# Twelve tile transposes go from TensorE to transfers on SyncE's queue, and one small product moves down the program order

## The chip, the cores and the metric

The kernel runs on one core of a Trainium2 chip. A core has five engines with instruction queues of their own: TensorE (PE in the profile, its weight loads PEld), VectorE (DVE), ScalarE (ACT), GpSimd (POOL) and SyncE (SP). Each queue is worked off in order; engines wait for one another through semaphores. Sixteen DMA engines move data between the large memory and the on-chip memory, or within the latter; SP, ACT and POOL only issue such transfers. TensorE writes to a small memory of eight banks (PSUM), from which VectorE or ScalarE copy. The metric is the device time of one execution in microseconds (us), less is better. Three executions before the change took 158.83, 157.96 and 158.57 us, with a median of 158.57.

## The reference

Two layers in a row, for 4 batches of 768 tokens, 8 heads of 64 and a model width of 512. The first is a recurrent attention with a decay per head:

```python
gamma = 1.0 - 2.0 ** (-5.0 - np.arange(H))
for t in range(S):
    state = gamma[None, :, None, None] * state + np.einsum('bhd,bhe->bhde', k[:, :, t], v[:, :, t])
    y[:, :, t] = scale * np.einsum('bhd,bhde->bhe', q[:, :, t], state)
```

Its output, with the heads side by side, is x of the second, a channel mix with a hidden width of 1024:

```python
xk = mu_k * x + (1.0 - mu_k) * x_prev      # x_prev: the token before
xr = mu_r * x + (1.0 - mu_r) * x_prev
k = np.maximum(xk @ w_k, 0.0)
v = k * k @ w_v
r = 1.0 / (1.0 + np.exp(-(xr @ w_r)))
return r * v
```

## The kernel before

The tokens are cut into 12 blocks of 256, three per batch: blocks 0 to 2 are batch 0, 6 to 8 batch 2, 9 to 11 batch 3. A block's attention is computed in chunks rather than token by token: masked scores of q and k inside a chunk, and products of q with the state carried from the chunks before. Blocks 0 to 5 use two chunks of 128 tokens, blocks 6 to 11 (`HALF`) four of 64.

The order of all work is written out by hand in `ORDER`. Each word is one step, `code.block.part`, with `~` the engine (v, a, p, s) and `@` the PSUM banks. The program emits the words from left to right, so each engine gets its instructions in that order. The words that matter here:

- `lq`, `lk`, `lv` load q, k, v of a block (`load`, lines 222 to 237, on POOL, which also casts q and k to 16 bits). They land in rings of four buffers, `Q16`, `K16`, `V32`, so a load waits until the block four places earlier has been read.
- `Tq`, `Tk` (`trans`, lines 264 to 283) transpose q and k on TensorE, so that the head's 64 features lie on the partitions. In blocks 6 to 11 that is 32 small products of 64x64 for each word (line 278). `Eq`, `Ek` (`turned_q`, `turned_k`, through `copy`, line 241) copy the outcome from PSUM to `QT`, `KT`, rings of three, on ScalarE.
- `S` scores (lines 310 to 343), `M` mask on VectorE (345 to 355), `C` the block's own states (357 to 399), `U` their sums with the carried state (`summed`, 419), `G` the decay (`decayed`, 421).
- `I`, `Y`, `J` the output products: `inter` (431 to 446, products at 441) with the carried state, called once for each half of the pairings, and `intra` with the masked scores (462, 478, 489). `HEADS` gives the pairs of heads that share the 128 partitions of `QT` and `KT`; the pairs (3, 2) and (7, 6) stand in turned order.
- `D` scales y into `xT` (507, 514), `dx` forms the differences of neighbouring tokens (529), `X` mixes them with the mu rows (538).
- `K` with `Qa`, `Qb`: the hidden layer on TensorE (552, 562) and its square on ScalarE (571, 579, 583). `V`: product with `w_v` (604). `R`, `s`: gate (592, 598). `O`: the result on VectorE into a ring of four `OS` buffers (610), `st`: its store on SP (617). An `O` therefore waits until the store of four half blocks earlier is done.
- `mu`, `mt`, `me`: the two mu vectors are loaded on ACT's queue (654), turned by one product on TensorE (`trans_mu`, 659), copied to `mu` on ScalarE (662).
- `z.n`: products of zeros (667, 674) that compute nothing.

Before the change SP's queue holds two early loads of block 0 and then only the 24 stores. The order around the start on TensorE is: the transposes of block 0, `mt`, two zero products, the first scores, the remaining k transposes, `C.0`, more scores, `Y.0`.

Of the kernel before, what the change touches and what calls it, by code (L numbers as in the profile page):

```python
# [33 lines left out]
X.1.1.3 X.1.1.2 Qb.1.0 Tq.3@1 Eq.3~a J.2 X.1.1.0 X.1.1.1 R.1.0@6 s.0.0 lk.3~p Tk.3@1 vs.3~v D.2~v
dx.2~v X.2.0.2 X.2.0.0 C.3@23 X.2.0.3 Ek.3~a s.1.0 X.2.0.1 lk.4~p U.3.0~a R.1.1@0 lq.4~p s.1.1
Tk.4@1 S.3.1@45 S.3.0@67 Qb.1.1 Qb.1.3 U.3.1 lv.4~p Tq.4@0 Ek.4~a Eq.4~a wv.0~p K.2.2@2 Qa.2.2
M.3.1~v K.2.0@3 Qa.2.0 G.3~a M.3.0~v K.2.3@1 vs.4~v Qb.0.3 S.4.1@45 S.4.0@67 M.4.0~v I.3@23
M.4.1~v Qa.2.3 lq.6~p lq.7~p K.2.1@0 Qb.2.0 Y.3 C.4@67 V.1.0.0@1 U.4.0 U.4.1 G.4~a I.4@45 J.3
Qa.2.1 D.3~v dx.3~v Y.4 V.1.1.0@6 Tq.7@23 J.4 D.4~v wv.1~p Qb.2.1 V.0.1.0@0 lk.6~p V.0.0.0@7
X.2.1.2 dx.4~v X.3.0.1 X.3.0.2 X.3.0.3 Eq.7~a V.1.1.1 X.3.0.0 V.0.0.1 O.0.0 Tk.6@45 Ek.6~a lq.5~p  # L40
Tq.6@23 lv.5~p Qb.2.2 V.0.1.1 Eq.6~a V.1.0.1 O.1.0 K.3.6@4 K.3.1@5 Qb.2.3 lk.5~p K.3.0@7 Qa.3.6
Tq.5@4 Qa.3.1 Qa.3.0 vs.5~v C.5@5 X.2.1.1 Eq.5~a Tk.5@1 Ek.5~a S.6@23 O.0.1 O.1.1 lk.7~p U.5.0
Tk.7@67 Ek.7~a X.2.1.0 I.5@45 M.6~v X.3.1.3 K.3.2@0 K.3.3@1 Qa.3.2 Qb.3.1 lv.6~p S.5.0@23 Qa.3.3
Qb.3.0 X.3.1.1 S.5.1@67 Qb.3.3 X.2.1.3 Qb.3.2 K.3.4@0 st.0.0 Qa.3.4 M.5.1~v lk.8~p K.3.5@1 Qa.3.5
R.2.1@6 lv.8~p lk.9~p s.2.1 M.5.0~v Y.5 S.7@23 Tk.8@01 Ek.8~a J.5 X.3.1.0 X.3.1.2 R.3.1@7 s.3.1
V.2.0.0@6 K.3.7@0 lv.7~p vs.6~v R.2.0@7 V.2.0.1 D.5~v M.7~v s.2.0 dx.5~v X.5.1.1 O.2.0 Qa.3.7
Qb.3.6 V.2.1.0@1 Tk.9@23 C.6@45 U.6.0~a Ek.9~a lq.8~p Tq.8@67 Qb.3.7 X.5.0.3 V.2.1.1 vs.7~v
R.4.0@0 Eq.8~a U.6.1 U.6.2 X.5.0.0 U.6.3 st.0.1 R.3.0@2 C.7@45 X.5.0.1 s.4.0 I.6@67 s.3.0 st.1.1
X.5.0.2 K.5.3@3 Qa.5.3 O.2.1 lq.10~p K.5.1@0 Qa.5.1 G.6~v X.5.1.3 V.3.0.0@1 U.7.0 U.7.1 U.7.2
st.2.1 I.7@23 Y.6 vs.8~v U.7.3 G.7~a lq.11~p R.4.1@0 D.6~v V.4.1.0@4 lv.11~p C.8@67 Y.7 V.3.1.0@5  # L50
Qb.5.1 Qb.3.4 Qb.3.5 V.3.0.1 dx.6~v s.4.1 U.8.0 U.8.1 V.3.1.1 Qb.5.3 D.7~v U.8.2 V.4.1.1 dx.7~v
X.6.0.1 X.6.0.3 V.4.0.0@7 K.5.0@6 X.5.1.2 X.6.0.2 Qa.5.0 V.4.0.1 Qb.5.0 K.5.2@0 X.6.0.0 Qa.5.2
Qb.5.2 X.6.1.2 lv.9~p K.6.7@6 Qa.6.7 st.2.0 st.1.0 O.4.1 O.3.0 K.6.0@2 Qa.6.0 lk.10~p O.4.0 O.3.1
st.3.1 K.6.4@0 S.8@67 I.8@23 Tk.10@45 Qa.6.4 K.6.1@1 Ek.10~a X.6.1.1 X.5.1.0 Qa.6.1 Qb.6.1 K.6.6@0
Qb.6.0 Qa.6.6 vs.9~v K.6.5@4 Qa.6.5 M.8~v R.5.1@1 Qb.6.6 Tq.10@67 Eq.10~a s.5.1 Y.8 Tq.11@45
Qb.6.7 lv.10~p vs.10~v X.6.1.3 Eq.11~a D.8~v dx.8~v lq.9~p X.8.0.2 X.8.0.1 lk.11~p R.5.0@0 s.5.0
K.6.3@6 Qa.6.3 V.5.1.0@7 Tq.9@23 X.6.1.0 Eq.9~a S.10@45 M.10~v Qb.6.3 C.9@01 U.9.0~v st.3.0 U.9.1
V.5.1.1 K.6.2@6 Qa.6.2 R.6.1@2 s.6.1 U.9.2 R.6.0@3 s.6.0 I.9@45 U.9.3 O.5.1 X.8.0.3 S.9@01 M.9~v
X.8.0.0 G.9~a C.10@67 U.10.0 U.10.1 Qb.6.2 vs.11~v R.7.1@2 s.7.1 V.5.0.0@3 Qb.6.5 st.4.1 Tk.11@01
Ek.11~a U.10.2 U.10.3 V.5.0.1 Qb.6.4 K.8.0@2 Qa.8.0 G.10~v I.10@01 Y.9 C.11@67 st.4.0 R.7.0@2  # L60
O.5.0 V.6.1.0@3 D.9~v U.11.0 U.11.1 s.7.0 K.8.3@4 Qa.8.3 V.6.1.1 U.11.2 I.11@67 st.5.0 dx.9~v
O.6.1 S.11@45 X.8.1.2 Y.10 V.7.1.0@2 M.11~v D.10~v dx.10~v X.9.0.3 X.9.0.2 X.9.0.1 V.7.0.0@3 Y.11
X.9.0.0 Qb.8.0 K.8.2@4 Qa.8.2 X.8.1.0 X.9.1.1 K.8.1@5 Qa.8.1 D.11~v V.6.0.0@0 V.7.0.1 V.6.0.1
K.9.3@1 K.9.7@5 Qa.9.7 X.8.1.1 V.7.1.1 X.8.1.3 dx.11~v K.9.2@4 O.7.0 Qb.8.1 Qb.9.7 O.6.0 Qa.9.3
st.5.1 Qa.9.2 X.11.1.0 Qb.8.3 X.11.0.3 K.9.1@5 K.9.4@6 st.7.0 Qa.9.1 Qb.9.1 R.8.0@1 s.8.0
V.8.1.0@3 Qb.9.2 X.9.1.0 K.9.0@0 Qa.9.0 Qb.8.2 X.9.1.2 Qb.9.3 K.9.6@1 Qa.9.6 Qb.9.6 O.7.1 st.7.1
K.9.5@7 Qa.9.5 V.8.0.0@0 X.11.0.2 X.11.0.1 Qb.9.0 X.11.0.0 K.11.3@2 K.11.0@1 Qa.11.3 st.6.1
R.8.1@5 V.8.1.1 X.11.1.2 Qa.9.4 st.6.0 X.9.1.3 R.9.1@2 R.10.1@4 R.10.0@6 V.8.0.1 O.8.0 s.8.1
K.11.1@5 Qb.9.4 s.10.0 V.9.0.0@7 V.9.1.0@0 Qa.11.1 Qb.11.1 O.8.1 Qb.9.5 Qb.11.3 Qa.11.0 st.8.1
K.11.2@6 Qa.11.2 V.10.1.0@5 Qb.11.2 Qb.11.0 V.9.1.1 R.9.0@1 X.11.1.3 s.9.0 X.11.1.1 V.9.0.1 O.9.0  # L70
st.9.0 V.11.0.0@6 s.10.1 s.9.1 O.9.1 st.9.1 V.10.0.0@1 V.10.1.1 O.10.1 st.8.0 st.10.1 V.11.0.1
R.11.0@0 s.11.0 O.11.0 V.10.0.1 R.11.1@7 s.11.1 O.10.0 st.10.0 Vc.11.1.1@0 Oc.11.1.1 Vc.11.1.0@6
st.11.0 sc.11.1.1~a Oc.11.1.0 sc.11.1.0~s
# [4 lines left out]
def kernel(  # L78
# [16 lines left out]
    P = 128  # L95
# [28 lines left out]
    gd_np = gam[np.array(HEADS).T[par // D]] ** TM  # L124
# [16 lines left out]
    Q16 = ring("q16_", 4, [H, 2 * D], F16)  # L141
    K16 = ring("k16_", 4, [H, 2 * D], F16)
# [16 lines left out]
    csm = const.tile([P, 4 * H + (2 + LOG) * NJ + 2 * NCO], F32, name="csm_sb")  # L159
# [14 lines left out]
    gd = csm[:, o : o + NJ]  # L174
# [22 lines left out]
    def heads(j):  # L197
        return [(a, h, h // 2, h % 2) for a, h in enumerate(HEADS[j])]

# [15 lines left out]
    def more(n):  # L215
        return n % NB < NB - 1

    def staged(a):
        f = K2(1 + a).rearrange("p f t -> p (f t)").bitcast(F32)
        return f[:, 0 : H * 2 * D].rearrange("p (h d) -> p h d", h=H)  # L220

    def load(x, d, split, a=None):
        def go(e, n, j0=0, j1=NJ):
            b, t0 = n // NB, n % NB * TM
            hs = slice(2 * j0, 2 * j1)
            src = x[b, hs, t0 : t0 + TM, :]
            dst = staged(a)[:, hs] if (a, n, j0) in EARLY else d(n)[:, hs]
# [536 lines left out]
```

## Time and profile before

| | |
|---|---|
| median of three executions | 158.57 us (157.96 to 158.83) |
| the profiled execution | 158.7 us from first to last instruction, its span |
| TensorE busy | 149.7 us, 94% |
| VectorE busy | 128.0 us, 81% |
| ScalarE busy | 98.9 us, 62% |
| GpSimd busy | 55.1 us, 35% (it issues the loads) |
| bytes moved by DMA | 22.29 MB, mean 140 GB/s |
| granted TensorE clock | mean 0.976 |

The profile is one execution; its times count from the span's start. Busy digits are tenths of a slice of about 4 us, 9 meaning 90% or more. The chain that ended last is followed back from the last instruction, each time to what released it, and shows which engine set the time in each stretch. A matmul's length includes its way through the array, so neighbouring matmuls overlap, and the distance from one group's start to the next one's tells what a group costs. The L numbers are lines of the kernel.

### The profile page before, as it was taken

Reading aid. Unit: us, or ns where it says so; the run is one execution under the profiler, and the core shown is the slowest. Engines: PE = TensorE matmul, PEld = TensorE weight load, DVE = VectorE, ACT = ScalarE, POOL = GpSimd, SP = SyncE. Lnnn points to the kernel's source line nnn. Section 1 sums busy time; section 2 is a strip of 40 time slices with the busy share of each in tenths; the row PEclk is TensorE's granted clock in tenths of the full one; section 3 lists DMA queues with packets and bytes.
Section 4 is the critical chain, followed back from the end, with each engine's and each line's share of the span. In section 5 each row is a group of like instructions: output and inputs, shape, how many; then the busy total and the mean of one; then the engine's idle time right before and its main releaser. Section 6 shows DMA issues by size and latency. Waiting matters only on the chain.

```text
span 158.7 us, 5316 instructions
## 1 busy us (share of the span) xinstructions
PE 149.7 (94%) x2316; PEld 85.5 (54%) x2316; DVE 128.0 (81%) x203; ACT 98.9 (62%) x182; POOL 55.1 (35%) x67
## 2 busy tenths in 40 slices
PE   7749989999999999999999999999999999999992
PEld 3334667765765445545654555555565445555451
DVE  2258799999999999999999999999999998040432
ACT  3437452989967479947662689978313498529330
POOL 7999426827967507702992000000000000000000
PEclk9985799999999999999999999999999999999998
DMA  5999999999999999990799934000300015001335
GB/s 151 273 181 175 203 244 243 162 238 182 182 201 179 218 215 175 192 171 9 170 316 216 98 121 150 4 6 0 136 6 4 0 66 197 1 0 70 130 135 198
DMA packets 44903, 22.29 MB, mean 140 GB/s; under 512 B 36424, under 2 KB 40400, under 8 KB 44880
## 3 DMA queue, kind: packets, MB, share of 16 engines
q0 software_dynamic: 39920, 14.95, 73.6%
q1 hardware_dynamic: 4512, 6.69, 11.7%
q10 hardware_dynamic: 448, 0.32, 0.7%
q8 instruction: 18, 0.29, 0.7%
q14 instruction: 5, 0.04, 0.1%
HBM read 24.31 MB, written 6.29 MB: 193 GB/s over the span
## 4 chain that ended last, share of the span: by engine, by line
PE 48%; DVE 31%; DMA 9%; issue 6%; ACT 4%; POOL 0%; DVEq 0%; POOLq 0%
PE ps L604 13%; PE ps L552 9%; PE ps L592 8%; DVE a L354 5%; PE ps L562 5%; DVE xk L538 4%; DVE xr L538 4%; DMA k<-in_k_dram 3%; DVE dx L529 3%; DMA mu<-in_moe_mu_r_dram 3%; DVE vs L253 3%; DVE tg L419 2%; DVE os L610 2%; DVE xT L507 2%; DMA k2s<-in_k_dram 2%
## 5 line engine op out<-in xcount | busy, mean ns | idle before, releaser
L604 PE MATMUL ps<-wv,k2s 128*128 128x512 f16 x184 | 44.4, 380 | 0.0
L571 ACT ACTIVATE kr<-ps 128x512 f32<-128x512 f32 x48 | 27.8, 597 | 21.6 <-PE ps L562 14.6
L604 PEld LDWEIGHTS <-k2s 128*128 128x128 f16 x184 | 17.3, 98 | 18.8
L610 DVE SCALAR_TENSOR_TENSOR os<-ps,rs 128x512 f32<-128x512 f32 x23 | 15.1, 685 | 14.4 <-PE ps L604 7.9
L592 PE MATMUL ps<-wr,xr 128*128 128x512 f16 x96 | 23.9, 380 | 0.0
L230 POOL DMA_DIRECT2D k<-in_k_dram x22 | 19.7, 915 | 12.1 <-PE ps L318 6.6
L562 PE MATMUL ps<-xk,wk 128*128 128x256 f16 x192 | 23.6, 273 | 0.2 <-DVE xk L538 0.2
L552 PE MATMUL ps<-xk,wk 128*128 128x512 f16 x96 | 22.6, 380 | 0.8 <-DVE xk L538 0.8
L598 ACT ACTIVATE rs<-ps 128x512 f32<-128x512 f32 x24 | 14.1, 602 | 13.9 <-PE ps L592 9.8
L230 POOL DMA_DIRECT2D v<-in_v_dram x22 | 19.8, 919 | 8.4 <-DVE vs L253 7.9
L562 PEld LDWEIGHTS <-wk 128*128 128x128 f16 x192 | 18.2, 98 | 4.8 <-DVE xk L538 0.5
L538 DVE SCALAR_TENSOR_TENSOR xr<-dx,mu,xT 128x256 f16<-128x256 f32 (+1 forms) x36 | 19.4, 569 | 0.0
L538 DVE SCALAR_TENSOR_TENSOR xk<-dx,mu,xT 128x256 f16<-128x256 f32 (+1 forms) x36 | 18.8, 568 | 0.2
L241 ACT COPY kT<-ps 128x1024 f16<-128x1024 f16 (+1 forms) x13 | 12.2, 951 | 9.3 <-PE ps L272 5.9
L253 DVE TENSOR_TENSOR vs<-v,csm_sb 128x1024 f16<-128x1024 f32 x12 | 14.6, 1219 | 3.1 <-DMA v<-in_v_dram 3.1
L354 DVE TENSOR_TENSOR a<-ps,c_sb 128x1024 f16<-128x1024 f32 (+1 forms) x14 | 14.4, 1067 | 1.9 <-PE ps L339 1.5
L552 PEld LDWEIGHTS <-wk 128*128 128x128 f16 x96 | 9.0, 98 | 12.1 <-DVE xk L538 1.1
L583 ACT ACTIVATE k2s<-kr 128x512 f16<-128x512 f32 x24 | 14.8, 632 | 0.2
L529 DVE TENSOR_TENSOR dx<-xT 128x1024 f32<-128x1024 f32 x12 | 14.7, 1222 | 0.2
L579 ACT ACTIVATE k2s<-kr 128x512 f16<-128x512 f32 x24 | 14.7, 628 | 0.1
L241 ACT COPY qT<-ps 128x1024 f16<-128x1024 f16 (+1 forms) x13 | 12.3, 952 | 3.5 <-PE ps L272 3.4
L592 PEld LDWEIGHTS <-xr 128*128 128x128 f16 x96 | 8.7, 98 | 9.7
(67 smaller groups left out, 157.8 us busy)
## 6 DMA issues: line engine op xcount, KB each, us to landing
out_dram<-os SPq DMA_DIRECT2D x23, 256.0 KB, 2.4
v<-in_v_dram POOLq DMA_DIRECT2D x22, 256.0 KB, 7.2
k<-in_k_dram POOLq DMA_DIRECT2D x23, 128.0 KB, 7.0
q<-in_q_dram POOLq DMA_DIRECT2D x11, 256.0 KB, 7.7
wk<-in_moe_w_k_dram POOLq DMA_DIRECT2D x2, 512.0 KB, 10.9
wv<-in_moe_w_v_dram POOLq DMA_DIRECT2D x2, 512.0 KB, 8.0
v<-in_v_dram POOLq DMA_DIRECT2D x1, 512.0 KB, 6.2
wr<-in_moe_w_r_dram POOLq DMA_DIRECT2D x1, 512.0 KB, 13.2
```

Of the source, the lines that this page charges most:

```text
L230: e.dma_start(out=dst[:, :, i * D : i * D + D], in_=src[:, i * P : i * P + P].rearrange("h p d -> p h d"),)
L241: e.copy(out=out, in_=in_)
L253: e.tensor_tensor(out=VS(n), in0=V32(n).rearrange("p h (i d) -> p i h d", i=2), in1=gks[:, int(half(n) or wide(n)), :, :, None].to_broadca ...
L354: nc.vector.tensor_tensor(out=a_full(n)[:, i, :, j0:j1], in0=pairs(banks("S", n, i, j0))[:, :, j0:j1], in1=(below if wide(n) else causal[: ...
L529: e.tensor_tensor(out=DX(k)[:, :, m * TM + t0 : m * TM + t1], in0=x[:, :, c + t0 : c + t1], in1=x[:, :, c - 1 + t0 : c - 1 + t1], op=ALU.s ...
L538: nc.vector.scalar_tensor_tensor(out=XM[w](k)[:, j, t0:t1], in0=DX(k)[:, j, t0:t1], scalar=mu[:, w * NCO + j : w * NCO + j + 1], in1=x[:, ...
L552: nc.tensor.matmul(banks("K", n, g), lhsT=wk16[:, co, g * P : g * P + P], rhs=XM[0](k)[:, co, :], start=(co == 0), stop=(co == NCO - 1),)
L562: nc.tensor.matmul(pz[:, i, :], lhsT=wk16[:, co, fo * P : fo * P + P], rhs=XM[0](k)[:, co, m * TM + t0 : m * TM + t1], start=(i == 0 and c ...
L571: nc.scalar.activation(out=kr, in_=banks("K", n, g, *u), func=AF.Relu)
L592: nc.tensor.matmul(banks("R", n, tb), lhsT=XM[1](k)[:, co, t : t + P], rhs=wr16[:, co, :], start=(co == 0), stop=(co == NCO - 1),)
L604: nc.tensor.matmul(banks("V", n, tb), lhsT=K2(n)[:, fo, tb * P : tb * P + P], rhs=wv16[:, fo, :], start=(fo == 0), stop=(fo == NFO - 1),)
L610: nc.vector.scalar_tensor_tensor(out=OS(2 * n + tb), in0=banks("V", n, tb), scalar=1.0 / (KSC * KSC), in1=RS(2 * n + tb), op0=ALU.mult, op ...
```

## The change

For blocks 6 to 11 (`SIDE`) the words `Tq`/`Eq` become `tq~s` and `Tk`/`Ek` become `tk~s`: one transposing transfer each, on SP's queue, from `Q16` or `K16` straight to `QT` or `KT`, without TensorE, PSUM or ScalarE. Each stands in the order where `Tq` or `Tk` stood. The transfer turns groups of 128 columns, so in these blocks a buffer holds, for each half i of the tokens, all heads side by side. The loads of q and k are therefore two transfers per block; for k that was so already, for q it was one. The head pairs of batches 2 and 3 become plain, (0, 1), (2, 3), and with them the decay table `gd`; since in plain order the first call of `inter` no longer touches every part of the bank, `intra_half` begins the missing ones. Where `Tq.7` stood there is one zero product, `z.1@2`. Apart from that, `mt` moves from before the first scores of block 0 to behind the last, just before `me`; everything else keeps its order.

```diff
-... Tk.0.0.2@0 mu Tq.0.2.4@1 cq.0.0.2~a z.2@6 Tq.0.0.2@2 Ek.0.0.2~a vs.0~v mt@3 Eq.0.0.2~a z.2@6 S.0.1.0.2@45
+... Tk.0.0.2@0 mu Tq.0.2.4@1 cq.0.0.2~a z.2@6 Tq.0.0.2@2 Ek.0.0.2~a vs.0~v Eq.0.0.2~a z.2@6 S.0.1.0.2@45
-S.0.1.2.4@01 me M.0.1.2.4~v lv.1~p
+S.0.1.2.4@01 mt@3 me M.0.1.2.4~v lv.1~p
-V.1.1.0@6 Tq.7@23 J.4 D.4~v ... Eq.7~a V.1.1.1 ... Tk.6@45 Ek.6~a lq.5~p Tq.6@23 lv.5~p ... Eq.6~a
+V.1.1.0@6 z.1@2 J.4 D.4~v ... tq.7~s V.1.1.1 ... tk.6~s lq.5~p lv.5~p ... tq.6~s
...
-K.6.1@1 Ek.10~a ... Tq.10@67 Eq.10~a s.5.1 Y.8 Tq.11@45 ... Eq.11~a D.8~v ... Tq.9@23 X.6.1.0 Eq.9~a S.10@45
+K.6.1@1 tk.10~s ... tq.10~s s.5.1 Y.8 ... tq.11~s D.8~v ... X.6.1.0 tq.9~s S.10@45
...
+PLAIN = ((0, 1), (2, 3), (4, 5), (6, 7))
+SIDE = (6, 7, 8, 9, 10, 11)
+PLAINB = (2, 3)
...
-    def heads(j):
-        return [(a, h, h // 2, h % 2) for a, h in enumerate(HEADS[j])]
+    def heads(j, n):
+        return [(a, h, h // 2, h % 2) for a, h in enumerate((PLAIN if n // NB in PLAINB else HEADS)[j])]
+
+    def natural(t, n, h, i):
+        if side(n):
+            return t[:, i * H * D + h * D : i * H * D + h * D + D]
+        return t[:, h * 2 * D + i * D : h * 2 * D + i * D + D]
...
+            if a is not None and side(n):
+                dst = d(n).rearrange("p (i h d) -> p i h d", i=2, h=H)
+                for i in range(2):
+                    e.dma_start(out=dst[:, i], in_=src[:, i * P : i * P + P].rearrange("h p d -> p h d"))
+                return
...
+    def flipped(a):
+        def go(e, n):
+            e.dma_start_transpose(
+                out=(KT if a else QT)(n).rearrange("c j i p -> c (j i) p"), in_=(K16 if a else Q16)(n)
+            )
+
+        return go
+
+    def tposed(a, n, s, j, i):
+        t = (KT if a else QT)(n)
+        if side(n):
+            return t.rearrange("c j i p -> c (j i) p")[low(s), i * NJ + j, :]
+        return t[low(s), j, i, :]
...
-                            pa[low(u), a, j, i, :], lhsT=KT(n)[low(a), j, i, low(u)],
-                            rhs=QT(n)[low(a), j, i, low(u)],
+                            pa[low(u), a, j, i, :], lhsT=tposed(1, n, a, j, i)[:, low(u)],
+                            rhs=tposed(0, n, a, j, i)[:, low(u)],
...
     def intra_half(n):
         py = pairs(banks("I", n))
+        fresh = [n // NB in PLAINB] * 2
...
-                    for a, h, jo, hp in heads(j):
+                    for a, h, jo, hp in heads(j, n):
+                        begin = hp == u and fresh[u]
+                        if begin:
+                            fresh[u] = False
...
-                            start=False, stop=False, skip_group_check=True,
+                            start=begin, stop=False, skip_group_check=True,
...
-        "Tq": trans(0), "Tk": trans(1), "Eq": turned_q, "Ek": turned_k,
+        "tq": flipped(0), "tk": flipped(1), "Tq": trans(0), "Tk": trans(1), "Eq": turned_q, "Ek": turned_k,
```

On SP's queue the order becomes: the two early loads, tq.7, tk.6, tq.6, tk.7, one store, tk.8, tk.9, tq.8, six stores, tk.10, tq.10, tq.11, tq.9, two stores, tk.11, and then the remaining stores.

More of the change, by code (lines that the diff above doesn't have):

```diff
@@ L158 @@
     c16 = const.tile([P, 4 * P + W], F16, name="c16_sb")
-    csm = const.tile([P, 4 * H + (2 + LOG) * NJ + 2 * NCO], F32, name="csm_sb")
+    csm = const.tile([P, 4 * H + (3 + LOG) * NJ + 2 * NCO], F32, name="csm_sb")
     gy = const.tile([P, NJ, TM], F32, name="gy_sb")
@@ L247, in go @@
             hs = slice(2 * j0, 2 * j1)
-            copy(e, (K16 if a else Q16)(n)[:, hs], staged(a)[:, hs])
+            copy(e, whole_d((K16 if a else Q16)(n), a)[:, hs], staged(a)[:, hs])
         return go
@@ L381, in state @@
                 for i in range(2 if more(n) else 1):
-                    for a, h, jo, hp in heads(j):
+                    for a, h, jo, hp in heads(j, n):
                         o = ps[low(a)]
@@ L392, in state @@
                 for u in range(2 if more(n) else 1):
-                    for a, h, jo, hp in heads(j):
+                    for a, h, jo, hp in heads(j, n):
                         o = ps[low(a)]
@@ L437, in inter @@
             for i in range(parts):
-                for a, h, jo, hp in heads(j):
+                for a, h, jo, hp in heads(j, n):
                     u = a ^ s
@@ L476, in intra @@
                 for i in range(2):
-                    for a, h, jo, hp in heads(j):
+                    for a, h, jo, hp in heads(j, n):
                         nc.tensor.matmul(
@@ L487, in intra @@
                 for u in range(2):
-                    for a, h, jo, hp in heads(j):
+                    for a, h, jo, hp in heads(j, n):
                         nc.tensor.matmul(
```

138 lines of the change are left out of this document (72 added, 66 removed).

## The prediction

> **What bounds the kernel now.** I read the page's busy times and slices first, then the chain that ended last, then the timeline of the stretches that the chain names.
>
> ```profile
> PE 149.7 (94%) x2316; PEld 85.5 (54%) x2316; DVE 128.0 (81%) x203; ACT 98.9 (62%) x182; POOL 55.1 (35%) x67
> ...
> DVE  2258799999999999999999999999999998040432
> ...
> PEclk9985799999999999999999999999999999999998
> DMA  5999999999999999990799934000300015001335
> ...
> PE 48%; DVE 31%; DMA 9%; issue 6%; ACT 4%; POOL 0%; DVEq 0%; POOLq 0%
> ```
>
> The first line gives each engine's busy time, the next ones 40 slices of 4 us in tenths. TensorE is busy 94% of the span, but VectorE's digits are 9 from slice 7 on until 130 us too, and the chain is shared by both (48% and 31%): from 20 to 90 us it runs almost wholly through VectorE, from 90 to 118.6 us through TensorE, then to 123.4 us through VectorE and through TensorE to the end. The DMA digits are 9 until 71 us, so what is added to the DMA engines before that meets traffic.
>
> The start is looser. In TensorE's timeline (start, length, group, in brackets the idle time before):
>
> ```profile
> 7.42 0.41 PE L272 MATMUL ps<-c_sb,q 128*64 128x128 f16 x8
> 9.92 0.20 PE L659 MATMUL ps<-csm_sb,mu 8*128 8x8 f32 x1 [2.09 <-DMA mu<-in_moe_mu_r_dram]
> ...
> 10.58 0.42 PE L339 MATMUL ps<-qT,kT 64*64 64x128 f16 x16
> ...
> 13.37 2.07 PE L667 MATMUL ps<-zero 128*128 128x512 f32 x2
> ```
>
> After the second q transposes of block 0 (from 7.42 us) TensorE waits 2.09 us for the mu rows, and the first scores (L339) stand behind it. The last line, one zero product of z.4, took 2.07 us; the next z.4, at 18.85 us, took 1.12. The stretches say why (busy time of PE, PEld, DVE, ACT, POOL, then the granted clock):
>
> ```profile
> 4.20:11.00 6.80, 3.96 (x50) 1.64 (x50) 2.17 (x4) 2.66 (x5) 6.80 (x9) 1.00 1.47 231
> 11.00:17.80 6.80, 6.70 (x129) 4.19 (x130) 5.09 (x7) 3.24 (x12) 5.64 (x7) 0.50 1.85 182
> ...
> 90.00:100.00 10.00, 9.86 (x228) 5.18 (x229) 9.73 (x15) 9.17 (x16) 0.00 (x0) 1.00 0.33 110
> 100.00:110.00 10.00, 9.85 (x240) 5.23 (x239) 9.69 (x16) 8.65 (x17) 0.00 (x0) 1.00 0.02 4
> 110.00:120.00 10.00, 10.00 (x278) 6.65 (x276) 9.62 (x17) 3.28 (x7) 0.00 (x0) 1.00 0.16 57
> ```
>
> In the 6.8 us up to 11.0 TensorE is busy for 3.96, and in the 6.8 us after it the clock is granted at 0.50. The three lower rows show VectorE busy 29.04 of 30 us while TensorE holds the chain: it could gain 0.96 us there and no more.
>
> **Part 1, the mu product goes behind the last scores of block 0.** Its operand lands at about 9.9 us and its reader, the copy to `mu` on ScalarE, is first needed by X.0.0.0 at 19.7 us; at its new place it waits for nothing and costs its 0.20 us. Its two small loads on ScalarE's queue stay where they are. The first scores then need the copied q, ScalarE's pair of 0.54 us copies from 7.87 us, so they start at 8.5 us instead of 10.58, 2.1 us earlier. VectorE's first mask is then held by its own `vs` product, which ends at 9.53, instead of starting at 11.05: 1.5 us. From there its work up to D.0 (two pairs of masks 1.29 each, one sum 0.42, `vs` of block 1 1.22, with small gaps) ends near 13.8, where D.0 started at 16.76: about 2.9 us. In between lay 1.45 us of waiting for TensorE at half clock, which shrinks because the products stand earlier even if the clock does not change. The gain lies between 0 (the next operand is as late) and 3.1 (clock stays full). Block 2's q lands only at 18.2 us while its transposes ran at 20.92, which allows 2.7. I take 2.6, near that last bound, because VectorE has no other free time after 18.1 us and whatever it starts earlier it keeps.
>
> The Trainium skill (TensorE: Matmul & The Clock Gate, Part 1) says the clock falls to half after a whole idle window of about 3.4 us. The rows show 2.84 us of idle in two pieces before the half clock, so the measurement does not bear out so long a gap; by the rule the clock need not depend on this wait at all, and the part would give 2.1.
>
> **Part 2, the transposes of blocks 6 to 11 leave TensorE.** Twelve groups of 32 small products go. From each group's start to the next group's they hold TensorE 0.26 to 0.43 us, 3.9 us in all. On the chain stand only the five after 90 us:
>
> ```profile
> 93.42 0.28 PE ps L278 x32
> ...
> 97.26 0.38 PE ps L278 x32
> ...
> 98.07 0.28 PE ps L278 x30
> ...
> 101.05 0.38 PE ps L278 x32
> ...
> 108.55 0.38 PE ps L278 x32
> ```
>
> That is 0.28 + 0.38 + 0.28 + 0.38 + 0.38 = 1.7 us; the seven before lie beside the full VectorE and give nothing. Added is one z.1 where Tq.7 stood at 49.2 us (0.39 us, no longer than what went and beside VectorE). The heads are paired in plain order in these blocks, so the products with the carried state (L441) meet only two of the four combinations of row half and output half, where the mixed pairs met all four and could overlap more; the trace has no such run. Their groups of 16 take 0.15 us; bounds are 0 and doubling, 8 groups after 90 us, so 0 to 1.2; half of it, 0.6, since weight loads already take part of that time. Net 1.1 us, of which VectorE lets through at most 0.96. I take 0.8, with bounds 0 and 1.0.
>
> ScalarE loses 12 copies of 1.02 us, 12.2 us; it carries 4% of the chain and I cost this at nothing. If that cover went, little more would come of it: the chain's ScalarE pieces all lie before 32 us, ahead of these copies. `intra_half` starting its own accumulations costs no instruction.
>
> **Part 3, the loads.** q of six blocks comes in two transfers instead of one: six more POOL issues of 0.92 us, 5.5 us, and 1024 more pieces each. POOL idles 6.65 us before 60.41 and 7.87 before 74.48, waiting for buffers, which hides them; without that cover the next to suffer is v of block 7, issued at 62.15, landing some 5.2 later, used at 72.96: 2.9 us to spare after the shift. Two of the issues stand ahead of block 6's k (38.26 us, 7.6 to landing): 47.7 instead of 45.9, still before SyncE wants it.
>
> **Part 4, twelve transposing transfers on SyncE's queue.** Their time T, from one to the next in this queue, is in no row. Each moves 256 KB within the on-chip memory, out of 1024 pieces of 256 bytes.
>
> ```profile
> out_dram<-os SPq DMA_DIRECT2D x23, 256.0 KB, 2.4
> ...
> k<-in_k_dram POOLq DMA_DIRECT2D x23, 128.0 KB, 7.0
> ```
>
> These lines give issues of one size and the median time to landing. Lower bound: a half load of k has as many such pieces, and two of them issued together land 0.9 us apart. Upper bound: 7.0 us, a busy k load, if each had to land before the next goes. Nearest is the first line, 256 KB on this very queue, so I take T = 2.4. The queue is in order, so every transpose and store waits for all ahead of it. These rows set the deadlines:
>
> ```profile
> 49.49 0.28 PE L441 MATMUL ps<-qT,tg 64*64 64x128 f16 x8
> ...
> 59.80 0.44 PE L318 MATMUL ps<-qT,kT 64*64 64x64 f16 x32
> ...
> 101.25 0.44 PE L318 MATMUL ps<-qT,kT 64*64 64x64 f16 x32
> ...
> 105.62 0.50 PE L318 MATMUL ps<-qT,kT 64*64 64x64 f16 x32
> ```
>
> (a) tq.7 overwrites what J.4 reads, which ends at 49.8; S.6 at 59.80 needs tq.7, tk.6 and tq.6. Both move by 2.6, so three transfers have 10.0 us: 7.2 used, nothing lost; late by 3T - 10.0. (b) Block 0's second store, issued at 59.3 until now, stands behind tk.8, tk.9 and tq.8. tq.8 waits for q of block 8, landed near 69 after the shift; the store lands at 69 + T + 2.4 = 73.8, just when O.2.1 (76.41 less 2.6) wants to overwrite its buffer, with all of VectorE's queue behind. No slack: late by T - 2.4. (c) tk.10, tq.10, tq.11, tq.9 stand behind the store of O.3.1, whose group ends at 93.1; S.9 at 105.62 needs the fourth. With 0.4 of part 2 gone that leaves 12.1: 9.6 used; late by 4T - 12.1. S.10 at 101.25 leaves 8.1 for two. tk.7 and tk.11 have 5 us and more, and block 3's first store behind tq.9 has 3 before O.5.0 at 111.3 wants its buffer. At T = 2.4 I cost the part at 0; at 0.9 also 0.
>
> Sum: 158.7 - 2.6 - 0.8 - 0 - 0 = **155.3 us**. The profiled span of 158.7 is 0.1 above the median of 158.57.
>
> **The rivals.** R1, slower: SyncE's queue becomes the bound, since each transfer is pushed tile by tile or must land first. For it speaks that busy transfers take 7 us; against it that the stores of this queue take 2.0 to 2.7 when the engines are quiet, as they are after 93 us. At T = 3.6, (a) is 0.8, (b) 0.4 more and (c) 2.3: the 3.4 us are eaten, and from there it is slower. At T = 4.5: (a) 3.5; SyncE is then busy until 78.7 us with tq.8, so (b) 3.8; (c) 5.9; 13.2 in all, so 168.5 us. At T = 7.0: 11.0 + 13.8 + 15.9 = 40.7, so 196 us. The Trainium skill (VectorE: DVE Perf Modes, The three transpose paths) gives 1309 ns for a 128x128 transpose by DMA; eight of them in series would be an estimate of 10.5 us per transfer and by the same sum about 235 us. The Trainium skill also has (DMA: Bandwidth & Descriptors, Latency and other measured facts) 261 GB/s for transposing transfers, an estimate of 1.0 us each and no loss. No run here shows either.
>
> R2, half hidden: T of 3.0 to 3.6, or the store of (b) is late by the time to landing seen among loads (up to 5.9 us, so 3.5 more): 157 to 159.5, say 158.
>
> R3, part 1 does nothing: another operand of block 0 is as late, and 158.7 - 0.8 = 157.9 is left. Against it speaks that q of block 0 is copied at 8.4.
>
> **How the numbers follow.** The forecast has 0.55, with its own range of 153 to 157: 3.1 + 1.0 at best leaves 154.6, and if VectorE's gaps between 20 and 90 us, 1.6 in all, closed as well, 153; 1.5 + 0.2 at worst gives 157. R1 0.30, R2 0.09, R3 0.06. Within 0.5% (0.8 us, about what can be told from no change) lies half of R2 and a little of R3: 0.06. Faster 0.62, slower 0.32. Below 152.8 I leave 0.04; above, R1 is cut at T near 4.8, 172 us, which leaves 0.16.
>
> **What would show it.** First scores at 8.5 us, full clock from 11 to 18 us, D.0 near 13.9. TensorE without waits for DMA at S.6, S.9 and S.10; VectorE without one at O.2.1. Issue to landing of the transposes under 5 us and 2.4 between two of them. I am wrong if TensorE waits for `qT` or `kT`, or if SyncE's queue is still at block 8 after 75 us.

## The result: 8.5% slower

The changed kernel takes 172.97 us in the median (170.50 to 173.29, four executions), the kernel before 158.7 (157.96 to 160.46). The ratio is 1.085, with a 95% interval from 1.073 to 1.098. The forecast was 155.3 us with a range up to 172.0: the sign was wrong and the time lies just above the range. The ratios in this text leave the disturbed executions of either kernel out, so a ratio is not always that of the two medians beside it.

The profiled execution took 173.13 us, with a span of 171.4. From the page after, busy times, slices of about 4.3 us, and the shares of the chain that ended last:

```profile
PE 150.2 (88%) x1933; PEld 84.9 (50%) x1933; DVE 128.5 (75%) x203; ACT 88.6 (52%) x170; POOL 60.4 (35%) x73
...
DVE  2497899999999401599949999999999999031440
...
PEclk9987999999999955599999999999999999999999
DMA  5999999999999999999999993997030003201334
GB/s 159 270 173 182 232 241 193 205 207 177 199 191 138 86 98 201 212 188 161 121 273 215 295 75 88 109 249 114 4 126 4 0 5 147 95 0 65 134 140 156
...
PE 43%; DVE 25%; DMA 16%; issue 6%; ACT 4%; SPq 2%; POOL 1%; DVEq 0%; POOLq 0%
```

VectorE's busy time is what it was, but its digits, which before were 9 without a break, fall to 4, 0, 1 and 5 in the 14th to 17th slice. In the last three of these the clock is at half. The DMA engines are full until 103 us, where before they were full until 71 and again from 79 to 91, and yet in slices 14 and 15 they move 86 and 98 GB/s, where the slices beside these show 138 and 201.

TensorE's first scores and first scores of block 6 (start, length, group, idle time before it):

```profile
7.91 0.42 PE L373 MATMUL ps<-qT,kT 64*64 64x128 f16 x16
...
67.23 0.64 PE L352 MATMUL ps<-qT,kT 64*64 64x64 f16 x32 [10.19 <-DMA qT<-q]
```

VectorE at D.0, at block 6's mask, at block 5's masks, and at O.2.1:

```profile
13.96 1.22 DVE L553 TENSOR_TENSOR xT<-ps,gy_sb 128x1024 f32<-128x1024 f32 x1 [1.00 <-ACT tg L459]
...
67.92 1.22 DVE L381 TENSOR_TENSOR a<-ps,c_sb 128x1024 f16<-128x1024 f32 x1 [10.18 <-PE ps L352]
...
72.69 2.35 DVE L388 TENSOR_TENSOR a<-ps,c_sb 128x1024 f16<-128x1024 f32 x2 [1.83 <-PE ps L365]
...
88.12 0.69 DVE L649 SCALAR_TENSOR_TENSOR os<-ps,rs 128x512 f32<-128x512 f32 x1 [2.27 <-DMA out_dram<-os]
```

The same four places in the trace before:

```profile
16.76 1.23 DVE L514 TENSOR_TENSOR xT<-ps,gy_sb 128x1024 f32<-128x1024 f32 x1 [1.45 <-issue]
...
60.47 1.22 DVE L347 TENSOR_TENSOR a<-ps,c_sb 128x1024 f16<-128x1024 f32 x1
...
63.32 2.35 DVE L354 TENSOR_TENSOR a<-ps,c_sb 128x1024 f16<-128x1024 f32 x2
...
76.41 0.68 DVE L610 SCALAR_TENSOR_TENSOR os<-ps,rs 128x512 f32<-128x512 f32 x1
```

The loss can be read off these lines as distances from D.0 (the spans end at 171.4 and 158.7):

| distance from D.0, us | before | after | loss so far |
|---|---|---|---|
| block 6's mask | 43.7 | 54.0 | 10.3 |
| block 5's masks | 46.6 | 58.7 | 12.2 |
| O.2.1 | 59.7 | 74.2 | 14.5 |
| end of the span | 141.9 | 157.4 | 15.5 |

D.0 itself stands 2.8 us earlier. So the span is longer by 15.5 - 2.8 = 12.7 us. The pieces are the wait of TensorE for block 6's transfers (10.3), a slow stretch behind it (1.9), a wait for a store (2.3), and 1.0 later. Of the last, 0.8 lies behind the last store: from its issue to the end of the span it is 3.5 us, 2.7 before. Its cause is open.

The transfers themselves, from the view of the tiles qT and kT (length of the issue on SyncE as min/median/max in ns, first and last start; then the time to landing):

```profile
L328 SPq DMA_TRANSPOSE qT<-q x6: 1232/1639/3786, 47.0 to 111.3; - x6
...
DMA to landing us min/median/max: 3.1/8.0/14.5
```

```profile
L328 SPq DMA_TRANSPOSE kT<-k x6: 1271/1358/3543, 49.1 to 113.8; - x6
...
DMA to landing us min/median/max: 4.4/8.9/15.0
```

One by one, in us: tq.7 from 47.0 to 59.9, tk.6 from 49.1 to 64.1, tq.6 from 52.7 to 67.2. The three between 110 and 114 us, when no load was under way any more, took 3.1 to 4.4. The same transfer is three to five times longer among the loads, and the loads suffer too: those issued between 47 and 54 us landed after 15 to 16 us, in the trace before after 6 to 7.5.

### The profile page after: what moved, and what is told of

It reads as the page before. It is cut to its first block, busy times and chain, and to the rows that moved or that the text cites. A ratio compares the mean times of both kernels' runs of the same rounds, so it can differ in the third digit from the quotient of the medians.

```text
span 171.4 us, 4579 instructions
## 1 busy us (share of the span) xinstructions
PE 150.2 (88%) x1933; PEld 84.9 (50%) x1933; DVE 128.5 (75%) x203; ACT 88.6 (52%) x170; POOL 60.4 (35%) x73
## 3 DMA queue, kind: packets, MB, share of 16 engines
q1 hardware_dynamic: 17184, 9.83, 29.3%
## 4 chain that ended last, share of the span: by engine, by line
PE 43%; DVE 25%; DMA 16%; issue 6%; ACT 4%; SPq 2%; POOL 1%; DVEq 0%; POOLq 0%
PE ps L643 12%; PE ps L591 10%; DMA qT<-q 8%; PE ps L631 6%; DVE a L388 6%; PE ps L601 5%; DMA out_dram<-os 4%; DMA v<-in_v_dram 3%; DVE xk L577 3%; DVE tg L453 3%; DVE dx L568 3%; SPq L328 2%; DVE xr L577 2%; DVE vs L273 2%; ACT k2s L622 2%
## 5 line engine op out<-in xcount | busy, mean ns | idle before, releaser
L591 PE MATMUL ps<-xk,wk 128*128 128x512 f16 x96 | 24.5, 403 | 1.1 <-DVE xk L577 0.9
L601 PEld LDWEIGHTS <-wk 128*128 128x128 f16 x192 | 18.2, 98 | 4.8 <-DVE xk L577 0.5
L591 PEld LDWEIGHTS <-wk 128*128 128x128 f16 x96 | 9.6, 102 | 13.3 <-issue 3.9
L388 DVE TENSOR_TENSOR a<-ps,c_sb 128x1024 f16<-128x1024 f32 (+1 forms) x14 | 14.4, 1063 | 2.2 <-PE ps L365 2.2
L381 DVE TENSOR_TENSOR a<-ps,c_sb 128x1024 f16<-128x1024 f32 x6 | 7.3, 1217 | 10.2 <-PE ps L352 10.2
L622 ACT ACTIVATE k2s<-kr 128x512 f16<-128x512 f32 x24 | 14.6, 630 | 0.2
L618 ACT ACTIVATE k2s<-kr 128x512 f16<-128x512 f32 x24 | 14.4, 622 | 0.1
L245 POOL DMA_DIRECT2D k<-in_k_dram x12 | 10.6, 888 | 9.2 <-DMA k<-in_k_dram 4.9
L245 POOL DMA_DIRECT2D q<-in_q_dram x12 | 10.6, 896 | 5.5 <-DMA k<-in_k_dram 4.4
```

The source lines that it names most:

```text
L245: e.dma_start(out=dst[:, i], in_=src[:, i * P : i * P + P].rearrange("h p d -> p h d"))
L388: nc.vector.tensor_tensor(out=a_full(n)[:, i, :, j0:j1], in0=pairs(banks("S", n, i, j0))[:, :, j0:j1], in1=(below if wide(n) else causal[: ...
L591: nc.tensor.matmul(banks("K", n, g), lhsT=wk16[:, co, g * P : g * P + P], rhs=XM[0](k)[:, co, :], start=(co == 0), stop=(co == NCO - 1),)
L601: nc.tensor.matmul(pz[:, i, :], lhsT=wk16[:, co, fo * P : fo * P + P], rhs=XM[0](k)[:, co, m * TM + t0 : m * TM + t1], start=(i == 0 and c ...
L622: nc.scalar.activation(out=K2(n)[:, w * g : w * g + w, t0:t1], in_=kr.rearrange("p a t -> p (a t)").rearrange("p (i t) -> p i t", i=w), fu ...
```

## The experiments

### Is it the mu product or the transposes?

`e_mt` is the kernel before with the mu product moved and nothing else; `e_turn` is the changed kernel with it moved back.

```diff
 # e_mt, from the kernel before
-... vs.0~v mt@3 Eq.0.0.2~a ... S.0.1.2.4@01 me M.0.1.2.4~v ...
+... vs.0~v Eq.0.0.2~a ... S.0.1.2.4@01 mt@3 me M.0.1.2.4~v ...
```

> The kernel before with the mu product moved and nothing else. In the changed kernel D.0 starts at 13.96 us instead of 16.76, and every stage up to 56 us runs 2.8 us earlier. If that gain is kept to the end when no transfer stands in its way, 158.7 - 2.8 = 155.9 us. If something later takes it back (VectorE or a load that comes no earlier), 158 to 159.

> The changed kernel with the mu product back before the first scores of block 0, so the transposing transfers alone. Theory: the first three transfers end when the DMA engines have worked off what is queued, about 67 us, whatever TensorE does before. Then the wait at the scores of block 6 shrinks from 10.2 to 7 or 8 us and the time is like the changed kernel's, 171 to 174 us. Rival: the wait is a fixed delay behind the transfer's issue, which follows J.4 of block 4; then it stays at 10 us and the time is 2.8 us more, 175 to 176.

`e_mt`: 156.59 us (156.04 to 158.51, ten executions) against 157.31, ratio 0.9964 (0.9931 to 0.9996). `e_turn`: 173.11 us, ratio 1.103 (1.090 to 1.116), with a wait of 8.9 us at block 6's first scores, between the 7 to 8 of the theory and the 10 of its rival. So the whole loss belongs to the transposes and what comes with them (the divided loads, the plain pairs), and the mu product is worth 0.6 us here instead of 2.6.

### Why the start gave so little: a second trace of the kernel before

`e_before` is the kernel before, unchanged. `e_start` is `e_mt` with four more single zero products where TensorE waits in the first 11 us.

```diff
 # e_start, from e_mt
-mu Tq.0.2.4@1 ... M.0.1.0.2~v Tk.0.2.4@2 ... U.0.1 S.0.0.2.4@67 M.0.0.2.4~v I.0@45
+mu z.1@6 Tq.0.2.4@1 ... M.0.1.0.2~v z.1@3 Tk.0.2.4@2 ... U.0.1 z.1@3 S.0.0.2.4@67 M.0.0.2.4~v z.1@3 I.0@45
```

> The kernel before, unchanged, for a second trace. Theory: the profiled execution that the prediction was read from had a stretch of half clock from 11.0 to 17.8 us that most executions lack; an execution with a mean clock of 1.00 has a span of 155.0 to 155.5 us, the same wait of 2.1 us before the mu product, D.0 near 13.5 instead of 16.76 and the q transposes of block 2 near 17.5 instead of 20.92. Then what the mu product's new place can give is 0.5 to 1 us and not 2.6. Rival: the 3.5 us between executions come from elsewhere, and the start looks as in the first trace, within 0.5 us.

> The kernel before with the mu product moved, and four single zero products put where TensorE waits in the first 11 us (before the q and the later k transposes of block 0, before its later scores and before its carried-state products). Theory (the half clock in a part of the executions follows from TensorE's idling at the start, and the mu product's new place matters mainly through that): nearly all executions keep a mean clock of 0.995 or more, where 14 of 37 of the kernel before and 2 of 10 with the mu product alone did not keep it; median 156.4 to 156.8 us. Rival (the half clock comes at random or from outside the core): the share of executions with half clock stays at 2 to 4 in 10, and the median at 156.6 or, with the zero products in the way, up to 157.2 us.

`e_before` took 157.67 us with a span of 155.9. Its stretches (busy time of PE, PEld, DVE, ACT, POOL, then the granted clock), and D.0:

```profile
4.20:11.00 6.80, 5.41 (x68) 2.20 (x70) 2.52 (x6) 2.72 (x5) 6.80 (x9) 1.00 1.50 233
11.00:17.80 6.80, 6.37 (x159) 3.80 (x156) 6.76 (x11) 5.06 (x13) 5.63 (x7) 1.00 1.85 182
```

```profile
14.56 1.22 DVE L514 TENSOR_TENSOR xT<-ps,gy_sb 128x1024 f32<-128x1024 f32 x1
```

The clock is full where it was half in the first trace, the wait for the mu rows is 1.39 us instead of 2.09, and D.0 stands at 14.56 instead of 16.76. The full clock is what the theory expected; a D.0 near 13.5 and a wait as long as before, which it expected too, did not come. From D.0 to the end both need nearly the same, 141.3 and 141.9 us. The trace that the prediction was read from was an execution with half clock at the start. In 80 executions of the kernel before, 37 had a mean clock of 0.995 or more (median 157.29 us), 35 of 0.979 or less (median 160.52), 8 lay between; the first trace, with half clock from 11.0 to 17.8 us, has 0.976.

`e_start`: 156.68 us (156.21 to 157.39), ratio 0.9938 (0.9902 to 0.9975). All twelve executions kept a mean clock of 0.997 or more; in the same set 11 of 17 executions of the kernel before had 0.989 or less, and so had 11 of 32 executions of the three kernels that move the mu product and have no transposing transfers before 60 us (`e_mt`, `e_late`, `e_pairs`). Its first stretches:

```profile
4.20:11.00 6.80, 6.64 (x101) 2.92 (x102) 3.52 (x7) 3.58 (x7) 6.80 (x9) 1.00 1.48 234
11.00:17.80 6.80, 6.50 (x139) 3.99 (x140) 6.74 (x9) 4.33 (x11) 5.66 (x7) 1.00 1.86 182
```

So TensorE's idling in the first 11 us brings the half clock on, and this version is faster than both kernels. How much idling it takes is open: 1.39 us in these 6.8 us left the clock full in `e_before`, and after 1.41 us in the traced `e_mt` came this stretch:

```profile
11.00:14.40 3.40, 3.40 (x48) 1.68 (x44) 2.37 (x4) 2.31 (x9) 3.37 (x5) 0.55 2.16 170
```

### Do the loads make the transfers late?

`e_nov` is the changed kernel without the loads of v of blocks 5 to 8, so these blocks compute with old values of v.

```diff
 # e_nov, from the changed kernel
-lv.5~p ... lv.6~p ... lv.8~p ... lv.7~p
```

> The changed kernel without the loads of v of blocks 5 to 8 (their products use v rows of earlier blocks that lie in the same buffers; the output of those blocks is wrong). Eight of the half loads that fill the DMA engines between 40 and 65 us are gone. Theory: the early transfers are slow because they share the engines with loads; then tq.7 lands 4 to 8 us after its issue instead of 12.9, the wait at the scores of block 6 falls from 10.2 us to 0 to 4, and the time to 157 to 163 us. Rival: a transposing transfer is slow by itself when three are queued; then it still waits 8 to 10 us and the time is 168 us or more.

It took 159.2 us, and TensorE's wait for `qT` and `kT` is gone. Tile qT in that trace:

```profile
L326 SPq DMA_TRANSPOSE qT<-q x6: 1232/1647/2331, 47.8 to 97.0; - x6
...
DMA to landing us min/median/max: 3.1/3.9/8.1
```

The transfers of blocks 6 and 7 landed after 8.1, 7.0, 4.6 and 3.1 us. Taking away 2 MB of loads beside them gives back 13.8 us, nearly the whole loss; this is one execution.

### Is it the bytes or the pieces?

`e_plain` puts a plain copy of the same 256 KB in the place of each transposing transfer.

```diff
-            e.dma_start_transpose(out=(KT if a else QT)(n).rearrange("c j i p -> c (j i) p"), ...
+            e.dma_start(out=(KT if a else QT)(n).rearrange("c j i p -> c (j i p)"), ...
```

> The changed kernel with every transposing transfer replaced by a plain copy of the same 256 KB between the same two buffers on the same queue (2 KB per partition instead of 256-byte pieces); q and k of batches 2 and 3 are then not turned, so that part of the output is not the reference's, while all work is still done. Theory one (bytes: any 256 KB added on the busy DMA engines waits its turn behind the loads): the copies of blocks 6 and 7 still take 9 to 15 us, the scores of block 6 wait 7 us or more, 168 to 173 us. Theory two (pieces: a transposing transfer is split into 1056 packets and pays for each among the loads): the copies land in 3 to 6 us also there, the wait at block 6 is under 1 us and the time is 157 to 159 us.

159.54 us (159.09 to 160.73), ratio 1.013 (1.009 to 1.017), 0.5 us above the range of theory two. q and k of these blocks are then not turned, but all work is done. Tile qT, then block 6's first scores, then O.2.1 in that trace:

```profile
L328 SPq DMA_DIRECT2D qT<-q x6: 465/534/559, 45.7 to 96.1; - x6
...
DMA to landing us min/median/max: 2.3/4.3/7.6
```

```profile
56.17 0.44 PE L352 MATMUL ps<-qT,kT 64*64 64x64 f16 x32 [0.43 <-DMA qT<-q]
```

```profile
74.13 0.69 DVE L649 SCALAR_TENSOR_TENSOR os<-ps,rs 128x512 f32<-128x512 f32 x1 [1.45 <-DMA out_dram<-os]
```

The bytes cost little: the copies of blocks 6 and 7 landed after 5.8 to 7.6 us, which is more than the 3 to 6 that theory two gave them, but in time. The loads beside them took 8 to 9.5 us, not 15 to 16. What makes the difference is the transposing form. The queue of these transfers counts 17184 packets in the changed kernel and 4512 before: 12672 more, 1056 for each transfer. Whether the number of pieces or the turning itself holds the DMA engines, this run does not separate. By the ratios it is still some 2.7 us longer than `e_mt`; the two waits shown are 1.9 of them.

### Which of the twelve cost?

Blocks 6 and 7 alone (`e_early`), 8 to 11 (`e_mid`), 9 to 11 (`e_late`); the other blocks are turned on TensorE, and the mu product is moved in all three.

```diff
-SIDE = (6, 7, 8, 9, 10, 11)
+SIDE = (6, 7)              # e_early;  (8, 9, 10, 11) in e_mid;  (9, 10, 11) in e_late
-PLAINB = (2, 3)
+PLAINB = (2,)              # e_early;  (2, 3) in e_mid;  (3,) in e_late
```

> Only blocks 6 and 7 turned by transfers (four instead of twelve), plus the mu product; blocks 8 to 11 are turned on TensorE as before. Theory (the transfers share the DMA engines with the loads that are waited for until about 70 us): these four carry the loss but for the late store, since no transposes of blocks 8 and 9 stand ahead of it: the first scores of block 6 wait 8 to 10 us, the clock falls to half after it, 164 to 168 us. Rival (the number of transfers on SyncE's queue is what counts): four of twelve cost a third, 160 to 163 us, and the wait at block 6 is under 5 us.

> Blocks 8 to 11 turned by transfers (eight instead of twelve), blocks 6 and 7 on TensorE, the store where the changed kernel has it, plus the mu product. Theory (the store's lateness is made by the loads that the transfers of blocks 6 and 7 slow down: q of block 8 lands at 78 us instead of 67): without those q of block 8 lands near 67, the store is issued by 70 and lands by 75, O.2.1 waits 0 to 3 us: 157 to 160.5 us. Rival (the order of SyncE's queue at block 8 costs its full amount by itself, because the transposes of block 8 and 9 are slow among the loads too): the wait at O.2.1 is 6 us or more, 163 to 168 us.

> The mu product moved, and only blocks 9 to 11 turned by transfers (issued after 90 us, when the loads have ended); blocks 6 to 8 on TensorE as before with the old head pairs. Theory: these six transfers land 3 to 4 us after issue and cost nothing, so the time is that of the mu product alone, or up to 1 us less for the 1.7 us of transposes that leave TensorE after 90 us: 155 to 156 us. Rival: the queue of SyncE is too slow for them too, and S.10 or S.9 waits: 158 us or more.

`e_early`: 167.88 us, ratio 1.067 (1.059 to 1.075); four of the twelve transfers carry some two thirds of the loss against `e_mt`. Block 6's mask in its trace:

```profile
66.20 1.23 DVE L380 TENSOR_TENSOR a<-ps,c_sb 128x1024 f16<-128x1024 f32 x1 [9.28 <-PE ps L351]
```

`e_mid`: 159.41 us (157.61 to 161.69), ratio 0.998 (0.993 to 1.004), no difference from the kernel before that can be told, though some 2.8 us more than `e_mt` had in its own set of executions. At a mean clock of 0.998 or more, five of its executions have a median of 158.91 us and two of the kernel before took 157.70 and 157.85, so about 1 us may be lost; two are too few to tell. The time is in the range of the theory. The traced execution, the longest of the ten, has a wait of 4.08 us at O.2.1, above the 0 to 3 of the theory; q of block 8 landed at 69.7 us, not at 78.

`e_late`: 157.66 us (156.37 to 159.78), ratio 1.000 (0.996 to 1.005), above the 155 to 156 that were expected. Its first transfer, k of block 9, is issued at 61.3 us, not after 90, and lands after 8.4; the others, from 89.6 us on, land after 3.1 to 4.9 us. Nothing waits for any of them. But nothing is won either. Two stretches of `e_late`, and the same two of `e_before`:

```profile
90.00:100.00 10.00, 9.90 (x152) 4.59 (x151) 9.69 (x13) 6.78 (x13) 0.00 (x0) 1.00 0.96 183
100.00:110.00 10.00, 9.33 (x199) 5.66 (x198) 9.52 (x19) 5.38 (x12) 0.00 (x0) 1.00 0.30 84
```

```profile
90.00:100.00 10.00, 10.00 (x322) 5.71 (x322) 9.69 (x14) 9.61 (x16) 0.00 (x0) 1.00 0.29 108
100.00:110.00 10.00, 9.85 (x231) 5.47 (x230) 9.55 (x18) 7.14 (x15) 0.00 (x0) 1.00 0.02 4
```

TensorE's busy time falls from 19.85 to 19.23 us, VectorE's stays at 19.2 of 20 and so does the pace: from block 8's D to block 9's it is 13.5 us in both.

### What do plain head pairs cost?

`e_pairs` has the mu product moved and plain pairs in batches 2 and 3, with all transposes on TensorE and the loads as before.

```diff
 # from the changed kernel, with the order of e_mt
-SIDE = (6, 7, 8, 9, 10, 11)
+SIDE = ()
```

> The kernel before with the mu product moved and, as the only other thing, the heads of batches 2 and 3 paired in plain order; all transposes stay on TensorE and all loads stay as they were. Theory: the carried-state products with plain pairs take 0.36 instead of 0.15 us per group of 16, 0.2 us more; of their groups those after 90 us are on TensorE's chain, 8 groups, so up to 1.6 us slower than the kernel with the mu product alone (156.6): 157.4 to 158.2 us, and this is what ate the gain of part 2 (1.7 us less, 1.6 us more). Rival: weight loads and VectorE hide it, and the gain of part 2 was never there: 156.6 us as with the mu product alone, within 0.3.

157.00 us (156.53 to 159.59), ratio 0.9974 (0.9937 to 1.0011). From D.0 to the end it is 141.4 us, in `e_mt` 141.3. The products do get slower, 0.36 us instead of 0.15 for a group of 16 in the changed kernel, and TensorE is busy 20.00 of the 20 us from 90 to 110; but VectorE sets the pace and hides it. The rival is right.

### The wait for the store, and the half clock

`e_st` moves block 0's second store ahead of tk.8. `e_warm` and `e_warm2` put 18 and 9 zero products before block 6's first scores. `e_fix` does both, with nine.

```diff
 # e_st, from the changed kernel
-S.7@23 tk.8~s ... U.6.3 st.0.1 R.3.0@2
+S.7@23 st.0.1 tk.8~s ... U.6.3 R.3.0@2
 # e_warm; z.36@2 in e_warm2 and e_fix
-Ek.5~a S.6@23
+Ek.5~a z.72@2 S.6@23
```

> The changed kernel with one word moved: block 0's second store goes ahead of the k transpose of block 8 on SyncE's queue. Theory (term (b): the store was late because it stood behind the transposes of block 8 and 9): VectorE's wait of 2.27 us before the result O.2.1 goes and 1.5 to 2.3 us with it: 170.7 to 171.5 us. Rival (the store is late because its own transfer is slow among the loads, or the next operand is as late): 173 us, with a wait of 1 us or more left at that place or at the next one.

> The changed kernel with 18 zero products (about 0.53 us each at full clock, 9.5 us in all) before the first scores of block 6, so that TensorE is busy while it waits for the transfers. Theory (the half clock from 59 to 73 us follows from TensorE's idling in that wait and costs about 2 us more): no half clock after the wait, the distance from block 6's mask to block 5's masks shrinks from 4.8 to about 2.9 us, and the kernel takes 171 us or a little less instead of 173. Rival (the clock falls for another reason, or the products end too late and delay the scores): half clock stays, or the scores move, and the time stays at 172.5 to 174 us.

> As the kernel with 18 zero products before the first scores of block 6, but with half as many: nine took 0.86 us each there, so 7.7 us, and end at about 64 us, before the last of the three transfers lands. Theory (half clock costs 1.9 us and the store behind the transposes of block 8 another 2.3): the scores of block 6 start when the transfer lands, the clock stays full, block 6's mask to block 5's masks takes 2.9 us instead of 4.8, and the time is 170.5 to 171.5 us. Rival: the time stays at 172.5 us or more because the transfers themselves end later or the store's wait grows by what was won.

> The changed kernel with both mends at once: block 0's second store ahead of the k transpose of block 8 on SyncE's queue, and nine zero products before the first scores of block 6. Theory (two limits stand one behind the other: the scores of block 6 wait for their transfers, and O.2.1 waits for the store behind block 8's transposes; each hides the mending of the other): with both gone only the lateness of the transfers of blocks 6 and 7 is left, about 8.5 us, and the kernel takes 165 to 167 us, against 168.2 with the store moved alone and 171.0 with the zero products alone. Rival (a third limit stands behind them, for instance q of block 8, which lands at 78 us): the time stays at 168 us or above.

`e_st`: 168.20 us (167.02 to 169.59), ratio 1.060 (1.055 to 1.066). O.2.1 has no wait left. The gain of 4.8, between medians of two sets, is twice what was expected; between the two traces (4.3 us) 2.3 is the wait, 0.9 an earlier D.0, 1.7 transfers of block 6 that landed earlier still, and 0.6 is lost again behind O.2.1.

`e_warm`: 173.93 us (172.87 to 175.22), as the rival had it: the zero products took 0.86 us each instead of 0.53 and ended long after the transfers had landed. The clock bears the theory out all the same. A stretch of the wait (clock in the third column from the right), then block 6's mask and block 5's:

```profile
60.00:68.00 8.00, 8.00 (x20) 3.57 (x19) 0.00 (x0) 0.00 (x0) 4.74 (x6) 1.00 1.68 155
```

```profile
72.74 1.23 DVE L380 TENSOR_TENSOR a<-ps,c_sb 128x1024 f16<-128x1024 f32 x1 [16.01 <-PE ps L351]
...
75.60 2.35 DVE L387 TENSOR_TENSOR a<-ps,c_sb 128x1024 f16<-128x1024 f32 x2
```

No half clock, and 2.86 us between the masks instead of 4.77. So the slow stretch follows from TensorE's idling in the wait, and it costs 1.9 us.

`e_warm2`: 170.97 us (170.37 to 173.62), with the traced execution the longest. There the scores start at 64.62 us, the clock holds, the masks are 2.9 us apart, and then:

```profile
88.65 0.69 DVE L648 SCALAR_TENSOR_TENSOR os<-ps,rs 128x512 f32<-128x512 f32 x1 [7.51 <-DMA out_dram<-os]
```

The median is the expected 2 us below the changed kernel's, but the two come from different sets, and the ratio to the kernel before is 1.085 for both, so a gain is not shown. In this execution there is none: the wait for the store has grown from 2.27 to 7.51 us and O.2.1 stands where it stood. Block 0's second store landed at 88.6 us, in the changed kernel at 88.0, although the scores of block 6 came 2.6 us earlier. It stands behind tq.8, tq.8 waits for q of block 8, and that landed at 78.7 us (78.0 in the changed kernel), because the loads are slow.

`e_fix`: 167.29 us (166.81 to 173.26), ratio 1.044 (1.038 to 1.049). Three of its four executions took 166.8 to 167.4 us, at or just above the upper end of what was expected; with both waits mended some 10 us stay. The fourth, the traced one, took 173.3: all transfers issued between 79.8 and 85.6 us, tq.8 among them, landed only after 13.8 to 16.2 us, and TensorE stood still for 6.15 us and VectorE for 5.54 behind it. What TensorE waited for there the trace doesn't name. The rival's third limit thus shows in one execution of four, and what brings it on stays open.

## Why the prediction was wrong

**The step that failed is the time T of a transposing transfer (part 4, 2.4 us).** It was taken from the stores on the same queue, as the "nearest" row, and the stores' median is made mostly in the quiet part of the kernel. The first three transfers start at 47 to 53 us, where the page before has the DMA engines at 9 of 10. There they took 12.9, 15.0 and 14.5 us to land. The prediction had noticed this ("what is added to the DMA engines before that meets traffic") and priced it only in the rival. Both signs of being wrong that the prediction names came: TensorE waits for `qT`, and SyncE's queue is at block 8 until 80.5 us. The model was wrong as well: it put the transfers one behind the other on the queue, T apart. They run side by side, issued 2 to 4 us apart, and land from 59.9 to 67.2 us, about when the loads issued beside them do (62.5 to 69.5 us). The distances of 3T and 4T have no counterpart in the trace.

**Term (a), "late by 3T - 10.0": the place was right, the size not.** S.6 waited 10.2 us for its transfers. `e_nov` and `e_plain` show the cause: loads beside them, and the transposing form.

**Term (b), "late by T - 2.4": right place, mostly for another reason.** It counted on q of block 8 at 69 us and a store landing in 2.4. They came at 78.0 us and took 7.4; the issue of tk.9, 3.5 us long, held the queue until 78.05 too. `e_mid` shows that without the early transfers q of block 8 lands at 69.7 us; what is left of (b) is at most the 2.8 us by which it is longer than `e_mt`. In the trace of `e_warm2` (b) alone, with the early transfers, holds O.2.1 at 88 us. How much of it stays in its shorter executions is not known.

**Term (c) was right at 0.** After 90 us the transfers land in 3.1 to 4.9 us, and `e_late` loses nothing by them.

**Part 1: right in the rows, wrong in the price.** The first scores were forecast for 8.5 us and came at 7.91, D.0 for 13.9 and came at 13.96. That D.0 fits so well is luck in part: the clock, forecast as full from 11 us on, was 0.59 from 11.0 to 14.4 us. And 2.6 us was counted from a D.0 at 16.76; in `e_before`, with full clock, it stands at 14.56, and in the trace of `e_turn`, with full clock and the product at its old place, at 13.69. The sentence "the profiled span of 158.7 is 0.1 above the median" hides the error: in the runs here the time is about 1.8 us more than the span (173.13 and 171.4, 157.67 and 155.9; 2.0 to 2.1 in `e_late`), so a span of 158.7 belongs to an execution of 160.5 us. The bounds of 0 and 3.1 held the 0.6 that `e_mt` measured, which R3 was nearer to. Beside it, half clock is what can be won at the start, and `e_start` took that.

**Part 2: 0 instead of 0.8.** The 0.96 us that VectorE "lets through" were the small gaps between its instructions, not waits; `e_late` freed 0.6 us of TensorE there and nothing moved. That the chain of waits names TensorE in a stretch does not make TensorE's time worth anything where VectorE is full beside it. For the same reason the plain pairs' cost, 0.6 in the sum, is 0.

**Part 3: no cost of its own was seen, but no run divides the loads alone.** `e_plain` has the divided loads, so what they cost lies within its 2.7 us. The six more issues fit, yet POOL lost its slack to something not in the sum: by the trace it waited up to 4.9 us for earlier loads of k to land before it issued the next, so slow loads also start later.

**The rivals.** R1 had the right sign and the right engine waiting, at a price that by its own sum would have been 168.5 us for T = 4.5. Its mechanism, that each transfer must land before the next goes, is not what happened. The estimate of 10.5 us for each transfer, worked out from the Trainium skill's 1309 ns for a 128x128 transpose by DMA (VectorE: DVE Perf Modes, The three transpose paths), is not borne out by the quiet transfers, which land after 3.1 us; and its 261 GB/s (DMA: Bandwidth & Descriptors, Latency and other measured facts) would make an estimate of 1.0 us for 256 KB, less than the 1.23 us that the shortest issue on SyncE took. Neither figure speaks of transfers among loads, which decided this case.

## What to carry to other kernels

Price an added transfer by rows from the stretch in which it will run, and by its form: here a transposing one landed with the loads around it where the DMA engines showed 9, and delayed these loads, so its bill came again further on. Before a profiled span is set against a median, compare that execution's own time and clock with the others. Work taken from one engine won nothing here where another engine beside it was full, whichever of the two the chain named.

## What was unexpected of the hardware

- A transposing transfer of 256 KB within the on-chip memory landed after 3.1 us when no loads were under way and after 12.9 to 15.0 us among loads; a plain copy of the same size took 2.3 us at the least and 5.8 to 7.6 among loads. While three of them were under way, the DMA engines showed as full and moved 86 GB/s. The issue alone holds SyncE for 1.23 us at the least and up to 3.8 among loads, a plain copy's for 0.47 to 0.56.
- TensorE stopped at 57.0 us, for 10.2 us, and the granted clock was half from 59.4 to 73.05 us. The Trainium skill (TensorE: Matmul & The Clock Gate, Part 1) lets the clock fall after a whole idle window of about 3.4 us. The traces do not agree: the clock fell 2.4 us after TensorE had stopped, in `e_turn` 3.3 and in `e_early` 2.0, and at the start of the traced `e_mt` it was 0.55 from 11.0 to 14.4 us after idle pieces of less than 0.5 us each.
- 35 of 80 executions of one and the same kernel had a mean clock of 0.979 or less and were 3.2 us longer in the median than those at full clock; with the mu product moved and four small products of zeros at the start, all twelve executions kept 0.997 or more.
